# Two layers of memory attention and a spatially gated MLP: the mixer's second tile on ScalarE, w_in's half stored by chunk, the bias rows loaded once, and four moves

## The chip, the cores and the metric

The kernel runs as one program on one core of one Trainium2 chip. The metric is the device time of that program in microseconds, the median of several executions. Beside it stands one profiled execution, whose span and instruction times the trace gives.

## The reference

Two layers, each an attention A and a mixer B, both with a layer norm ahead and a residual sum behind. S = 2048 rows, D = 640, 32 heads of 20, four segments of 512 rows, F = 1728.

```python
# A: per segment s, causal attention inside the segment, plus a memory of the earlier ones
a_dot = softmax(qs @ ks.T * scale + mask) @ vs
a_mem = (phi(qs) @ M) / (phi(qs) @ z + 1e-6)
o     = sigmoid(beta) * a_mem + (1 - sigmoid(beta)) * a_dot
M, z  = M + phi(ks).T @ vs, z + phi(ks).sum(0)
x = x + concat(o) @ wo

# B
z = gelu(layernorm(x) @ w_in)              # 2048 x 1728
z1, z2 = z[:, :864], layernorm(z[:, 864:])
g = w_sp @ z2 + b_sp[:, None]              # w_sp is 2048 x 2048
x = x + (z1 * g) @ w_out
```

## The kernel before

Every float32 matrix product is made of three float16 products: each operand is scaled by a power of two and split into a high and a low half (`split_scaled`, `split_t`), and TensorE adds high x high, high x low and low x high. The scales come from maxima over the weights; `pow2_parts` takes them through TensorE (a transpose `wtp`, then a broadcast `wbc`).

A layer has three stages. **Attention** (0 to some 618 us, and 1183 to 1736) works through pairs of heads, segment by segment: logits (`mp`, `es`), exponentials `P` on ScalarE, their halves `PH` (ScalarE) and `PL` (GpSimd, L1286), products `pv`. Between them run the projections of the tiles to come and, at the end, the output projection `yps` of tiles 0 to 11, whose sum with x is taken out of PSUM by VectorE (L1051). The tiles of x go through `prep(t)`: a load, the statistics, the normalisation, the transpose. **Phase 1b** (618 to 823, 1736 to 1926) takes the 16 row tiles in the order `ORDER` = 0, 8, 1, 9, ...: for tiles 12 to 15 the output projection `yp`, then layer norm, a DMA transpose to `th`, and the two halves of w_in (`zp0` with `wi`, whose result is z1, and `zp1` with `wi1`, whose result is z2). ScalarE takes gelu (L400, L423), VectorE normalises z2, and sums and differences of halves of z2 go to `zh` and `zl`. **Phase 2** (823 to 1180, 1926 to 2277) computes w_sp @ z2 for pairs of row blocks p and p + 8 with seven products in place of eight, after Strassen and Winograd: `gc`, `ga`, `gd`, `gb` are their PSUM banks, `product(ps, q, j, start)` is one product with 24 matmuls, "12", "11", "22", "21" are blocks of w_sp and s1 to s4 sums of them. GpSimd makes the sums (`summed`, L611), ScalarE and VectorE split them (`split`), and ScalarE copies a bank with the bias `bsp` as an addend (`copy`, L708). `gate`, `turn` and `tail` do z1 * g and the product with w_out.

Layer 0 also prepares what layer 1 reuses: split weights are stored to DRAM (`keep`), and the blocks of w_sp's first pair are split during phase 1b (`Rows.first`) and stored as `w0`; `fetch` loads them at the start of phase 2 in both layers. `rows.load(q)` loads the rows of w_sp of one pair, `rows.scales(q)` makes their scales.

Every DMA is issued on SyncE's queue (SP), one after the other: an issue that waits for its data holds all behind it. The order of instructions on each engine comes from a scheduler which follows the code, priorities (`high_priority`) and bounds (`issue_after(x)`: not before x); in phase 2 the order of the four compute engines is that of the code (`manual_schedule`). Each engine then works strictly in that order and waits where data or a buffer is missing.

The lines which the change and the prediction touch: L292 normalises a tile on VectorE, L365 and L366 do the first half of it for tile 0 on VectorE (the negated mean) and ScalarE (x minus mean), and L375 and L376 apply the factor while they split; L335 and L338 load tiles, L377 and L300 transpose them; L162 stores a weight; L468 loads w_sp's rows, L599 is the fetch, L569 loads the bias, L496 and L497 split w_sp's blocks.

Of the kernel before, what the change touches and what calls it, by code (L numbers as in the profile page):

```python
# [20 lines left out]
NT = S // 128  # L21
# [55 lines left out]
def split_scaled(g, h, l, st, c):  # L77

    nc = g.nc
    iv = g.iv[:st.shape[0], c:c + 1]  # L80
    nc.scalar.activation(h, st, AF.Identity, scale=iv)
    nc.vector.scalar_tensor_tensor(l, st, iv, h, ALU.mult, ALU.subtract)

# [84 lines left out]
def prologue(g, ctx, wv, wq, wk, wo, w_in, w_out):  # L168

    nc, tc = g.nc, g.tc  # L170
    wp = ctx.enter_context(tc.tile_pool(name="wqkv", bufs=1))
    g.w = {}
    g.wo = Weight(g, "o", 3, wo, 0, D)
    g.wi = [Weight(g, "i0", 4, w_in, 0, FH), Weight(g, "i1", 5, w_in, FH, FH)]
    g.wu = Weight(g, "u", 6, w_out, 0, D)
    with tc.tile_pool(name="wpro", bufs=1, side="right", reuse_waits="tile") as p, \
            tc.tile_pool(name="wpp", bufs=1, space=PSUM, reuse_waits="tile") as pp:
        st = p.tile([128, KD, D], F32, name="wstv")
        for k in range(KD):
            nc.sync.dma_start(st[:, k, :], wv[k * 128:(k + 1) * 128, :])  # L180
        with tc.high_priority(offset=HP):
            am = p.tile([128, KD], F32, name="wamk")
            for k in range(KD):
                nc.vector.tensor_reduce(am[:, k:k + 1], st[:, k], AX.X, ALU.max, apply_absolute_value=True)
            nc.vector.tensor_reduce(g.wam[:, 0:1], am, AX.X, ALU.max)
            g.vscale = pow2_scales(g, p, pp, "wsc", g.wam, 0, 1)
        g.w["v"] = [wp.tile([128, KD, D], F16, name=f"wv{x}") for x in "hl"]
        g.wqk = {nm + x: nc.dram_tensor(f"w_{nm}{x}", (128, KD, D), F16, kind="Internal").ap() for nm in "qk" for x in "hl"}
        for k in range(KD):
            split_scaled(g, g.w["v"][0][:, k], g.w["v"][1][:, k], st[:, k], 0)  # L190
    g.qk_w = wq, wk
# [53 lines left out]
def other_scales(g, stage, pool, psum, tag):  # L245
# [18 lines left out]
    yield False  # L264
    yield False
    parts = pow2_parts(g, pool, psum, tag, g.wam, 3, 4)
# [49 lines left out]
def phase1b(g, o_d, x, x1_d, z1_d, zh, zl):  # L316

    nc, tc = g.nc, g.tc
    with ExitStack() as ctx:
        pool = lambda n, b, **k: ctx.enter_context(tc.tile_pool(name=n, bufs=b, reuse_waits="tile", **k))  # L320
        pe2, pe1, pe3 = pool("be2", 2), pool("be1", 1), pool("be3", 3)
        wp0, px1, p2, px2, p3 = pool("bw0", 1), pool("bx1", 1), pool("b2", 1), pool("bx2", 1), pool("b1", 3)
        pz1, py, pz0 = pool("bz1", 2, space=PSUM), pool("by", 1, space=PSUM), pool("bz0", 1, space=PSUM)
        g.wi[0].paired(wp0)
        wi0 = g.wi[0].load(g.prep[0], 864, "wr")
# [18 lines left out]
        def attn_out(t, *a):  # L344
# [14 lines left out]
            xn = pe1.tile([128, D], F32, tag="xn", name="xn")  # L359
            if t:  # L360
                layernorm(g, x1, xn, D, 2, XS)
# [69 lines left out]
        for i, t in enumerate(ORDER):  # L431
            if i == 8:
                with tc.issue_after(g.loaded[ORDER[i]].ins):
                    g.wi[0].keep()
            if i + 1 < NT:
# [8 lines left out]
            th = th1  # L444
        z1_half(ORDER[-1], w_in_half(0, *old))
        g.rows = Rows(g)
        if not g.wsp_scaled:
# [107 lines left out]

def phase2(g, b_sp, x1_d, z1_d, zh, zl, out):
    nc, tc = g.nc, g.tc
    KO = 7
    NP = NT // 2
    with ExitStack() as ctx:  # L560
# [6 lines left out]
        woh, wol = g.wu.tiles(wp)  # L567
        bsp = wp.tile([128, NT], F32, tag="bsp", name="bsp")
        nc.sync.dma_start(bsp, b_sp.rearrange("(t p) -> p t", p=128))  # L569
        kn = [128] * 6 + [FH - 768]  # L570
# [21 lines left out]
        def fetch():  # L592
# [3 lines left out]
            with tc.high_priority(offset=HP), tc.issue_after(g.stored.ins):  # L596
                for nm in ("12", "11", "22", "s2", "s1", "s3", "s4"):
                    for c in range(2):
                        nc.sync.dma_start(blocks[0, nm, c], g.w0[nm, c])  # L599

# [87 lines left out]
        bank = lambda nm: pg.tile([128, 512], F32, tag=nm, name=nm)[:, :FHH]  # L688
        fetch()
        with tc.issue_after(g.loaded[ORDER[NT - 1]].ins):  # L690
            rows.load(1)
# [10 lines left out]
        for p in range(NP):  # L702
# [13 lines left out]
            if p:  # L716
                held = gate(over, z1)
                over = turn(p - 1, over, *held)
                split(p, "s1")
                if not q:  # L720
                    split(p, "s4")

# [25 lines left out]
            if p + 2 < NP:  # L748
                rows.load(p + 2)
            if p and q:  # L750
                split(p, "s4")
# [139 lines left out]
class Attention:  # L891
# [78 lines left out]
    def prep(self, t):  # L970
# [7 lines left out]
        def behind():  # L978
            ctx = ExitStack()
            for e in g.hold[:2] if t > 1 else ():  # L980
                ctx.enter_context(self.tc.issue_after(e.ins))
# [368 lines left out]
    def run(self, nseg=NSEG):  # L1350
# [6 lines left out]
        def early():  # L1357
            for t in range(0, 4, 2):

                with self.tc.high_priority(offset=HP if t == 0 else 0):  # L1360
                    for f in zip(self.prep(t), self.prep(t + 1)):
                        f[0]()
# [78 lines left out]
        def background():  # L1441
# [3 lines left out]
            if not g.wo.made:  # L1445
                for i, _ in enumerate(other_scales(g, self.bg, self.pl1, self.pm, "ms")):
                    yield 5 + i if _ else 8 + i
            yield 45
# [81 lines left out]
def interleaved_layers(ctx, tc, x, wq, wk, wv, wo, beta, w_in, w_sp, b_sp, w_out, out):  # L1530
# [4 lines left out]
    attn_consts(g, cp, beta)  # L1535
    prologue(g, ctx, wv, wq, wk, wo, w_in, w_out)

    def dram(name, shape, dt=F32):
# [5 lines left out]
    g.st = [dram(f"st{i}", (D, 3, 2, L), F16) for i in range(2)]  # L1544
    g.w_sp = w_sp
    g.w0 = {(nm, c): dram(f"w0{nm}{c}", (128, 2, 4, 128), F16) for nm in WB for c in range(2)}
    g.hold = ()
    x = rows(x)
    for layer in range(2):
# [5 lines left out]
        with ExitStack() as zs:  # L1555
            with tc.tile_pool(name="topo", bufs=1, side="right", reuse_waits="tile") as to, \
# [7 lines left out]
                phase1b(g, o_d, x, x1_d, z1_d, zh, zl)  # L1564
            phase2(g, b_sp, x1_d, z1_d, zh, zl, x2)
        x = x2
# [26 lines left out]
```

## Time and profile before

| | us |
|---|---|
| median of 3 executions | 2274.4 (2271.16 to 2276.78) |
| the profiled execution | 2279.19 |
| its span in the trace | 2277.5 |
| TensorE busy | 2107.4 |
| VectorE, ScalarE, GpSimd busy | 1606.0, 1250.7, 1458.3 |

The profiled execution is 4.8 us above the median, and 1.7 us of it lie outside the span. The rows of the page that show busy time, and the waits of TensorE, stand in the prediction. A row of the timeline gives start, length, engine, line, operation, and in brackets the idle time just before it with what ended that time; a row of waits gives who waited for whom, the total, how often, and the longest. The granted clock is the share of full speed that TensorE's throttle allowed in a stretch.

### The profile page before, as it was taken

To read this page: it belongs to the slowest core of one execution; us is meant where nothing else is said; L and a number is where in the kernel's file an instruction comes from. 1 tells how busy PE (TensorE), PEld (TensorE's weight loads), DVE (VectorE), ACT (ScalarE), POOL (GpSimd) and SP (SyncE) were. 2 spreads that over 40 slices of the span, in tenths; PEclk is the share of its full clock that TensorE was granted. 3 is DMA by queue.
4 is the path that set the end of the run, shared out by engine and by line. 5 is a ranking of instruction groups with operands and counts; after the bars stand their busy time and mean duration, and the time that the engine had idled before them with its cause. 6 is when DMAs were issued, how large, how long until landed. Compare 5 with 4: busy or idle time off the path is not lost.

```text
span 2277.5 us, 53085 instructions
## 1 busy us (share of the span) xinstructions
PE 2107.4 (93%) x21322; PEld 1266.8 (56%) x21322; DVE 1606.0 (71%) x2761; ACT 1250.7 (55%) x1639; POOL 1458.3 (64%) x1300
## 2 busy tenths in 40 slices
PE   5888888999899989999998998999998999999998
PEld 3455555666554545555554556556664555555555
DVE  7688678677687658878845777786776765576563
ACT  3578688888643433333314887888884333333331
POOL 2387788999844426647611889999996443475560
PEclk9999899999999999999999999999999999999999
DMA  5665557444676678777654447543445336877763
GB/s 164 161 159 157 141 156 174 125 115 124 159 189 180 170 215 208 167 162 187 159 146 117 106 117 178 124 122 89 121 128 149 91 109 197 189 187 174 167 149 84
DMA packets 539639, 342.79 MB, mean 151 GB/s; under 512 B 413536, under 2 KB 465248, under 8 KB 539392
## 3 DMA queue, kind: packets, MB, share of 16 engines
q1 hardware_dynamic: 539392, 339.40, 58.3%
q8 instruction: 167, 2.74, 0.5%
q14 instruction: 80, 0.66, 0.1%
HBM read 159.19 MB, written 92.55 MB: 111 GB/s over the span
## 4 chain that ended last, share of the span: by engine, by line
PE 48%; DVE 16%; POOL 10%; DMA 9%; ACT 8%; issue 6%; SPq 2%; ACTq 0%; DVEq 0%; POOLq 0%
PE zp L387 9%; PE ga L641 9%; POOL PL L1286 6%; PE cyp L677 5%; PE qps L1072 3%; PE pv L1314 3%; PE vps L1013 3%; PE mp L1211 2%; PE kps L1072 2%; PE gb L641 2%; DVE mxs L1275 2%; PE gc L641 2%; ACT PH L1284 2%; PE gd L641 2%; PE es L1211 1%
## 5 line engine op out<-in xcount | busy, mean ns | idle before, releaser
L1286 POOL TENSOR_TENSOR PL<-P,PH 128x640 f16<-128x640 f32 x384 | 539.1, 1429 | 56.0 <-PE pv L1314 44.8
L1275 DVE TENSOR_REDUCE mxs<-mp 128x2 f32<-128x1024 f32 (+2 forms) x384 | 320.5, 862 | 150.0 <-PE mp L1202 148.1
L1249 ACT ACTIVATE P<-es,sc 128x1024 f32<-128x1024 f32 (+1 forms) x256 | 271.3, 1060 | 102.0 <-PE es L1202 91.9
L387 PEld LDWEIGHTS <-th 128*128 128x128 f16 x1920 | 188.1, 98 | 179.7 <-DMA th<-xnhl 11.4
L611 POOL TENSOR_TENSOR ts<-ts,wt 128x512 f32<-128x512 f32 x196 | 280.1, 1440 | 11.1 <-DMA wt<-wn 0.2
L1284 ACT CAST PH<-P 128x1280 f16<-128x1280 f32 x192 | 239.6, 1248 | 1.5
L641 PEld LDWEIGHTS <-wts 128*128 128x128 f16 x1536 | 151.2, 99 | 145.1 <-issue 18.6
L641 PE MATMUL ga<-zh,wts 128*128 128x432 f16 x768 | 214.1, 351 | 11.3 <-ACT u L708 11.2
L286 POOL TENSOR_TENSOR lnrs<-lnve,mhalf 128x1 f32<-128x1 f32 x96 | 60.1, 634 | 247.5 <-DVE lnve L285 234.7
L387 PE MATMUL zp<-wi,th 128*128 128x432 f16 x960 | 183.7, 350 | 5.7 <-ACT z L423 5.7
L1286 POOL TENSOR_TENSOR PL<-Pb,PH 128x640 f16<-128x640 f32 x124 | 175.4, 1438 | 16.0 <-PE pv L1314 14.9
L611 POOL TENSOR_TENSOR ts<-wt,wt 128x512 f32<-128x512 f16 x28 | 34.7, 1241 | 230.6 <-DMA wt<-wn 230.6
L1013 PE MATMUL vps<-wvh,xt 128*128 128x320 f16 x640 | 153.9, 308 | 28.9 <-DVE relu L1104 23.6
L641 PEld LDWEIGHTS <-wt 128*128 128x128 f16 x1152 | 112.5, 98 | 99.6 <-DMA wt<-w 3.3
L677 PE MATMUL cyp<-wuh,ut 128*128 128x320 f16 (+1 forms) x896 | 163.7, 299 | 3.9 <-DMA ut<-un 3.9
L1314 PE MATMUL pv<-vs,PL 128*128 128x41 f16 x2560 | 157.5, 182 | 9.7 <-POOL PL L1286 9.6
L1211 PEld LDWEIGHTS <-qk 64*128 64x128 f16 (+1 forms) x2048 | 78.6, 94 | 155.8 <-issue 135.7
L677 PEld LDWEIGHTS <-ut 128*128 128x128 f16 (+1 forms) x1344 | 131.1, 98 | 58.7 <-DMA ut<-un 5.2
L1314 PE MATMUL pv<-vs,PH 128*128 128x41 f16 x2560 | 160.1, 183 | 0.4 <-DVE ab L1330 0.4
L387 PE MATMUL zp<-wi1h,th 128*128 128x432 f16 x640 | 149.5, 348 | 7.9 <-DMA th<-xnhl 7.6
L1211 PE MATMUL es<-qk 64*128 64x512 f16 (+3 forms) x1024 | 124.8, 300 | 24.6 <-ACT P L1249 20.0
L1314 PEld LDWEIGHTS <-PL 128*128 128x128 f16 x2560 | 140.7, 97 | 11.5 <-POOL PL L1286 11.4
(220 smaller groups left out, 5292.9 us busy)
## 6 DMA issues: line engine op xcount, KB each, us to landing
qk<-st SPq DMA_DIRECT2D x256, 120.0 KB
wr<-in_B_w_sp_dram SPq DMA_DIRECT2D x60, 512.0 KB
z<-z SPq DMA_DIRECT2D x32, 432.0 KB
cz<-z SPq DMA_DIRECT2D x32, 432.0 KB
xt<-in_A_x_dram SPq DMA_DIRECT2D x32, 320.0 KB
st<-qhl SPq DMA_DIRECT2D x40, 256.0 KB
st<-khl SPq DMA_DIRECT2D x40, 256.0 KB
x<-x SPq DMA_DIRECT2D x32, 320.0 KB
```

Of the source, the lines that this page charges most:

```text
L387: nc.tensor.matmul(zp[:, n, :FHH], a[:, k, :], b[:, k, c:c + FHH], start=(k == 0 and j == 0), stop=(k == KD - 1 and j == 2))
L611: nc.gpsimd.tensor_tensor(t, a, t if b == "t" else get(b), ALU.add if op == "+" else ALU.subtract)
L641: nc.tensor.matmul(ps, w[:, a, k % 4, :], z[:, k, j, :], start=start and k == 0 and i == 0, stop=k == NP - 1 and i == 2, skip_group_check= ...
L677: nc.tensor.matmul(yp[:, n, :320], a[:kn[k], k, :], b[:kn[k], k, n * 320:(n + 1) * 320], start=(k == 0 and j == 0), stop=(k == KO - 1 and ...
L1013: nc.tensor.matmul(ps, a[:, k, c], b[:, k, n * 320:(n + 1) * 320], start=(i == 0), stop=(i == 14))
L1072: nc.tensor.matmul(ps, a[:, k, c], b[:, k, :], start=(i == 0), stop=(i == 14))
L1211: nc.tensor.matmul(out[:, h, o:o + w], a[r, ac], b[r, bc], start=o == 0, stop=False, skip_group_check=True)
L1249: g.exp = nc.scalar.activation(P, E, AF.Exp, scale=g.esc)
L1275: e = nc.vector.tensor_reduce(mx[:, :, n, j], mp[:, :, o:o + w], AX.X, ALU.max)
L1284: nc.scalar.copy(PH, P[:, h])
L1286: (nc.gpsimd if h == 0 or n < self.N - self.TAIL else nc.vector).tensor_tensor(PL[:, c], P[:, h, c], PH[:, c], ALU.subtract)
L1314: nc.tensor.matmul(pv[:, i, h, :], x[:, c:c + 128], v[:, j, h0 + h, :], start=(j == 0 and x is PH), stop=(j == i and x is PL), skip_group_ ...
```

## The change

The line numbers of the new kernel are up to 8 higher.

- **Second tile on ScalarE.** In phase 1b, tile 8 takes the way of tile 0: VectorE makes only the negated mean, ScalarE subtracts it, and the factor is applied in the split. Both layers.
- **w_in's half by chunk.** Layer 0 stored w_in's first half in two DMAs behind the ninth tile of the order. Now each of its five chunks of 128 rows is stored (two DMAs each) at the ninth to thirteenth tile.
- **Bias rows once.** `bsp` is loaded once into the constants, instead of in phase 2 of each layer; the code has the load in layer 0's phase 1b, and the order has it as the ninth DMA of the program.
- **Fetch first.** `rows.load(1)` is bound behind the fetch's fourth DMA; SP's order has it behind all fourteen.
- **Last sum's split.** In the last pair, s4 is split where the other pairs have it, behind the copies, instead of ahead of them.
- **Scales' transposes.** `other_scales` yields once less, and its two transposes come some hundred TensorE rows earlier in layer 0's attention.
- **The start.** wv's loads get the priority of x's first tile; `prep(0)` goes ahead of `prep(1)` in layer 0; the statistics of tiles 2 and 3 are bound behind wv's third split.

```diff
@@ prologue
-        for k in range(KD):
-            nc.sync.dma_start(st[:, k, :], wv[k * 128:(k + 1) * 128, :])
+        with tc.high_priority(offset=HP):
+            for k in range(KD):
+                nc.sync.dma_start(st[:, k, :], wv[k * 128:(k + 1) * 128, :])
...
-            split_scaled(g, g.w["v"][0][:, k], g.w["v"][1][:, k], st[:, k], 0)
+            e = split_scaled(g, g.w["v"][0][:, k], g.w["v"][1][:, k], st[:, k], 0)
+            if k == 2:
+                g.third = e
@@ other_scales
     yield False
-    yield False
     parts = pow2_parts(g, pool, psum, tag, g.wam, 3, 4)
@@ phase1b
+        if not g.wsp_scaled:
+            nc.sync.dma_start(g.bsp, g.b_sp.rearrange("(t p) -> p t", p=128))
...
-            if t:
+            if t not in ORDER[:2]:
                 layernorm(g, x1, xn, D, 2, XS)
                 return xn, None
...
-            if i == 8:
+            if 8 <= i < 8 + KD and not g.wi[0].made:
                 with tc.issue_after(g.loaded[ORDER[i]].ins):
-                    g.wi[0].keep()
+                    g.wi[0].keep_chunk(i - 8)
...
+        g.wi[0].made = True
@@ phase2
-        bsp = wp.tile([128, NT], F32, tag="bsp", name="bsp")
-        nc.sync.dma_start(bsp, b_sp.rearrange("(t p) -> p t", p=128))
+        bsp = g.bsp
...
-                        nc.sync.dma_start(blocks[0, nm, c], g.w0[nm, c])
+                        e = nc.sync.dma_start(blocks[0, nm, c], g.w0[nm, c])
+                    if nm == "11":
+                        two = e
+            return two
...
-        fetch()
-        with tc.issue_after(g.loaded[ORDER[NT - 1]].ins):
+        two = fetch()
+        with tc.issue_after(g.loaded[ORDER[NT - 1]].ins), tc.issue_after(two.ins):
             rows.load(1)
...
                 split(p, "s1")
-                if not q:
-                    split(p, "s4")
...
-            if p and q:
+            if p:
                 split(p, "s4")
@@ attention
-            for e in g.hold[:2] if t > 1 else ():
+            for e in (g.hold[:2] or (g.third,)) if t > 1 else ():
...
-                    for f in zip(self.prep(t), self.prep(t + 1)):
+                    with self.tc.high_priority(offset=HP if t == 0 and not self.g.wo.made else 0):
+                        a = self.prep(t)
+                    for f in zip(a, self.prep(t + 1)):
...
-                    yield 5 + i if _ else 8 + i
+                    yield 5 + i
```

How the order moves at three places. First VectorE at the end of layer 0's attention (`xn` is tile 8 normalised, `xt` the drain of `yps`), before:

```order
L1051 SCALAR_TENSOR_TENSOR xt<-yps,sc,xt 128x320
L1325 TENSOR_TENSOR rs<-pv,iomg 128x8
L1326 RECIPROCAL rs<-rs 128x8
L1330 TENSOR_TENSOR ab<-pv,rs 128x328
L292 TENSOR_SCALAR xn<-x_11531,lnmv,lnrs 128x640
L1051 SCALAR_TENSOR_TENSOR xt<-yps,sc,xt 128x320
L1286 TENSOR_TENSOR PL<-Pb,PH 128x640 x2
```

and now:

```order
L369 TENSOR_SCALAR neg<-lnmv 128x1
L1056 SCALAR_TENSOR_TENSOR xt<-yps,sc,xt 128x320
L1330 TENSOR_TENSOR rs<-pv,iomg 128x8
L1331 RECIPROCAL rs<-rs 128x8
L1335 TENSOR_TENSOR ab<-pv,rs 128x328
L1056 SCALAR_TENSOR_TENSOR xt<-yps,sc,xt 128x320
L1291 TENSOR_TENSOR PL<-Pb,PH 128x640 x2
```

The normalisation of tile 8 between the attention's `ab` and the drain is gone; a negation of one column stands earlier, behind the statistics.

Second SP in the middle of layer 0's phase 1b (`w_i0h` and `w_i0l` are the stored halves, `th` the transposed tile), before:

```order
L468 DMA wr<-in_B_w_sp_dram 128x2x512 x2
L424 DMA z_0_9<-z_12017 128x864
L335 DMA x_12187<-x_0_4 128x640
L162 DMA w_i0h<-wi_11498 640x1x864
L162 DMA w_i0l<-wi_11498 640x1x864
L300 DMA_TRANSPOSE th<-xnhl 128x10x128
```

and now:

```order
L473 DMA wr<-in_B_w_sp_dram 128x2x512 x2
L428 DMA z_0_9<-z_12021 128x864
L339 DMA x_12191<-x_0_4 128x640
L152 DMA w_i0h<-wi_11500 128x864
L152 DMA w_i0l<-wi_11500 128x864
L302 DMA_TRANSPOSE th<-xnhl 128x10x128
L345 DMA_TRANSPOSE o<-o_3 128x10x128
L428 DMA z_0_2<-z_12129 128x864
L362 DMA x_0_12<-x_12375 128x640
```

The two whole stores ahead of the transpose have become one chunk's. On TensorE the product of the next tile's `th` with `wi1` (30 matmuls) now stands ahead of the product with `wi` of the tile before; it stood behind 26 of its 30 matmuls.

Third ScalarE in the last pair of layer 0's phase 2 (`wts` are split sums, `u` the copies), before:

```order
L618 CAST wts_16390<-ts_16230 128x512
L665 ACTIVATE un<-u,uivw 128x864
L618 CAST wts_16440<-ts_16259 128x512
L618 CAST wts_16443<-ts_16262 128x512
L618 CAST wts_16446<-ts_16227 128x512
L618 CAST wts_16449<-ts_16230 128x512
L708 ACTIVATE u<-ga,bsp,wsc 128x432 x4
```

and now:

```order
L625 CAST wts_16400<-ts_16240 128x512
L672 ACTIVATE un<-u,uivw 128x864
L625 CAST wts_16450<-ts_16269 128x512
L625 CAST wts_16453<-ts_16272 128x512
L715 ACTIVATE u<-ga,bsp,wsc 128x432 x2
L625 CAST wts_16578<-ts_16237 128x512
L625 CAST wts_16581<-ts_16240 128x512
L715 ACTIVATE u<-ga,bsp,wsc 128x432 x2
```

The second pair of casts (s4) has moved behind two of the copies.

More of the change, by code (lines that the diff above doesn't have):

```diff
@@ L81, in split_scaled @@
     nc.scalar.activation(h, st, AF.Identity, scale=iv)
-    nc.vector.scalar_tensor_tensor(l, st, iv, h, ALU.mult, ALU.subtract)
+    return nc.vector.scalar_tensor_tensor(l, st, iv, h, ALU.mult, ALU.subtract)
 class Weight:
@@ L553, in first, with phase2 @@
         store("s4", 0, 1)
-def phase2(g, b_sp, x1_d, z1_d, zh, zl, out):
+def phase2(g, x1_d, z1_d, zh, zl, out):
     nc, tc = g.nc, g.tc
@@ L1536, in interleaved_layers @@
     prologue(g, ctx, wv, wq, wk, wo, w_in, w_out)
+    g.bsp = cp.tile([128, NT], F32, name="bsp")
     def dram(name, shape, dt=F32):
@@ L1544, in interleaved_layers @@
     g.st = [dram(f"st{i}", (D, 3, 2, L), F16) for i in range(2)]
-    g.w_sp = w_sp
+    g.w_sp, g.b_sp = w_sp, b_sp
     g.w0 = {(nm, c): dram(f"w0{nm}{c}", (128, 2, 4, 128), F16) for nm in WB for c in range(2)}
@@ L1564, in interleaved_layers @@
                 phase1b(g, o_d, x, x1_d, z1_d, zh, zl)
-            phase2(g, b_sp, x1_d, z1_d, zh, zl, x2)
+            phase2(g, x1_d, z1_d, zh, zl, x2)
         x = x2
```

## The prediction

> **What bounds the kernel now.** I read the page first (busy time and the slices), then the waits of TensorE, then its granted clock in the stretches behind the longest waits, and last the timelines of the places that the change touches.
>
> ```profile
> span 2277.5 us, 53085 instructions
> PE 2107.4 (93%) x21322; PEld 1266.8 (56%) x21322; DVE 1606.0 (71%) x2761; ACT 1250.7 (55%) x1639; POOL 1458.3 (64%) x1300
> ```
>
> TensorE works 2107.4 of 2277.5 us, so some 170 us are its idle time, and no edit here takes matmuls away. A saving can only come from its waits, and from the clock behind them. The waits, by what ended them:
>
> ```profile
> PE ga L641 <- ACT u L708: 11.2, 9, 3.8
> ...
> PE yps L1045 <- DVE xt L1051: 8.5, 2, 5.4
> ```
>
> Columns: total us, times, longest. These two groups are 19.7 us in 11 waits; the change touches their longest ones, and single waits of other groups shown below at their places. Behind several of them TensorE also runs slowly (start:end, length, busy, granted clock, DMA share, GB/s):
>
> ```profile
> 612.00:618.00 6.00, 4.32 (x46) 0.72 0.57 154
> 693.50:701.00 7.50, 7.42 (x27) 0.65 0.90 226
> 823.00:827.50 4.50, 4.42 (x25) 1.00 1.05 392
> 845.00:851.00 6.00, 5.92 (x24) 0.72 0.47 87
> 1137.00:1144.30 7.30, 7.14 (x26) 0.63 0.01 2
> 1727.00:1733.00 6.00, 5.13 (x55) 0.51 0.80 166
> ```
>
> Length times (1 - clock) is what the slow clock cost there: 1.7, 2.6, 0, 1.7, 2.7 and 2.9 us. The wait before 823 was 2.85 us (its row stands below) and left the clock at 1.00; those before the others were 3.08 to 5.67 us. So a long wait that is removed returns about 2 us beyond its length.
>
> [...]
>
> **Second tile centred on ScalarE, layers 0 and 1.**
>
> ```profile
> 603.40 9.77 DVE L292 TENSOR_SCALAR xn<-x,lnmv,lnrs 128x640 f32<-128x640 f32 x1 [0.32 <-POOL lnrs L286]
> 609.65 2.75 POOL L1286 TENSOR_TENSOR PL<-Pb,PH 128x640 f16<-128x640 f32 x2
> 613.68 0.42 PE L1045 MATMUL yps<-woh,o 128*128 128x320 f16 x1 [3.08 <-DVE xt L1051]
> 615.99 1.42 SPq L377 DMA_TRANSPOSE th<-xnhl  x1
> 620.22 0.90 PE L387 MATMUL zp<-wi1h,th 128*128 128x432 f16 x2 [1.81 <-DMA th<-xnhl]
> 1716.96 10.40 DVE L292 TENSOR_SCALAR xn<-x,lnmv,lnrs 128x640 f32<-128x640 f32 x1 [1.69 <-POOL lnrs L286]
> 1727.87 0.42 PE L1045 MATMUL yps<-woh,o 128*128 128x320 f16 x1 [5.45 <-DVE xt L1051]
> 1729.77 2.76 POOL L1286 TENSOR_TENSOR PL<-Pb,PH 128x640 f16<-128x640 f32 x2 [0.53 <-PE pv L1314]
> L292 DVE TENSOR_SCALAR xn<-x,lnmv,lnrs x30: 606/612/10396, 603.4 to 1909.9; 128x640 f32<-128x640 f32 x30
> L366 ACT ACTIVATE xn<-x,neg x2: 828/830/833, 537.0 to 1654.8; 128x640 f32<-128x640 f32 x2
> ```
>
> The same normalisation that takes 0.61 us in the median took 9.77 and 10.40 us for tile 8, while GpSimd ran one subtraction after the other, and it ended when they did. The PSUM drain L1051 stood behind it on VectorE, and TensorE waited for that. The change replaces it by L366 on ScalarE (0.83 us) and a tiny negation on VectorE. ScalarE's 0.83 us stands in its queue of exponentials and casts; it worked 55% of the span, and GpSimd's chain, not ScalarE, ends last there: I take 0, bound 0.8 a layer, its own length.
>
> In layer 0 the wait of 3.08 us goes, but GpSimd's own chain still runs to 612.4, and tile 0's transpose was issued at 615.99 and ended TensorE's wait 4.2 us later. TensorE had been ready for the drain at 610.6 (613.68 - 3.08). With the drain at about 611 and the transpose, behind two more drains' stores, at about 613, the first w_in matmul starts near 617 in place of 620.2: 3.1 us, plus some of the clock. I take 3.5 (2 to 5.5). In layer 1 GpSimd's last part began at 1729.77, since it waited for a `pv` behind the same stall; it can begin near 1727, when GpSimd had no other work left (the 10.40 us end at 1727.4), so 2.8 us earlier. The drains and the last `pv` behind it ran at half the clock for 2.9 us of loss, which goes too, less a little: attention ends about 5.3 us earlier (3.5 to 6.5). Next late there: GpSimd's subtractions.
>
> **w_in's half stored by chunk.**
>
> ```profile
> 682.15 1.44 SPq L162 DMA_DIRECT2D w_i0l<-wi  x1
> 683.70 6.74 SPq L300 DMA_TRANSPOSE th<-xnhl  x1
> ...
> 693.58 7.41 PE L387 MATMUL zp<-wi,th 128*128 128x432 f16 x26 [5.67 <-ACT z L423]
> ```
>
> Two stores of 1080 KB (the row is the second) stand ahead of the transpose, whose issue then took 6.74 us. TensorE stood in front of the first-half product of the tile before, which waits for ScalarE's L423. Now one fifth of the stores stands there, and TensorE's order has the second-half product of the next tile first, which needs only the transpose. That lands near 690 (bounds 688 to 691: 683.7, the 4.2 us above, and what the stores and loads still ahead take), and that product covers L423: 26 matmuls took 7.41 us, 4.8 without the slow clock, so its 30 take 5.6. The stall cost 5.67 + 2.6 = 8.3 us; about 2.1 stay; gain 6.2 (3 to 8). The other eight issues on SP are at most 1.4 us each (1.44 above, for five chunks) and go past loads of tiles to come; one pair goes ahead of w_in's last load, which that delays by its issue: 0, bound -1.
>
> **Bias once, and the fetch ahead of the rows.**
>
> ```profile
> 812.80 2.78 SPq L468 DMA_DIRECT2D wr<-in_B_w_sp_dram  x3
> 815.62 4.37 SPq L599 DMA_DIRECT2D wt<-w  x6
> 823.08 0.36 PE L641 MATMUL gc<-zh,wt 128*128 128x432 f16 x1 [2.85 <-DMA wt<-w]
> ...
> 822.38 1.22 DVE L480 TENSOR_REDUCE am<-wr 128x1 f32<-128x1024 f32 x1
> ...
> 827.20 2.56 ACT L496 ACTIVATE wn<-wr,wsc 128x512 f16<-128x512 f32 x4 [1.12 <-DMA wts<-w0s]
> ...
> 844.32 0.71 ACT L708 ACTIVATE u<-ga,bsp,wsc 128x432 f32<-128x432 f32 x1 [9.46 <-DMA bsp<-in_B_b_sp_dram]
> 845.08 0.34 PE L641 MATMUL ga<-zh,wts 128*128 128x432 f16 x1 [3.21 <-ACT u L708]
> ```
>
> With the fetch some 2.8 us earlier and no w_sp megabytes before it, the 2.85 us go. ScalarE's copy waited 9.46 us for the bias alone: 3.21 us of TensorE and 1.7 of clock, 4.9. What is late next is the copy's place on ScalarE: four casts of w_sp stand ahead of it, and their rows now load behind fourteen fetch issues. The fetch, fourteen blocks of 128x1024 in 2 bytes, is 3.7 MB, which at the 392 GB/s of the row at 823 is 9.4 us; the rows, 2.1 MB, 5.3 us more, so from 812.8 they land near 829, some latency included. Before, the last reduction of the rows began at 822.38 and the casts were through at 829.8, 7.4 us later; so now near 837. TensorE, without its 2.85 and 3.21 us, asks for the copy's result at 845.1 - 6.1 = 839.0, so for its start by 838. I keep 4.9 (bounds 2.5 and 5). In layer 1, of the 11.2 us of `ga <- ACT u`, little can be here: 3.21 and the 3.79 below are layer 0's, and the other seven are 4.2 together. I take 0.5 (0 to 1).
>
> **Last sum's split.**
>
> ```profile
> 1130.29 1.12 ACT L618 CAST wts<-ts 128x512 f16<-128x512 f32 x2
> ...
> 1135.88 0.62 ACT L618 CAST wts<-ts 128x512 f16<-128x512 f32 x1 [2.51 <-POOL ts L611]
> 1136.41 0.70 ACT L708 ACTIVATE u<-ga,bsp,wsc 128x432 f32<-128x432 f32 x1
> 1137.16 0.52 PE L641 MATMUL ga<-zh,wts 128*128 128x432 f16 x1 [3.79 <-ACT u L708]
> ```
>
> The copy stood behind casts that wait for GpSimd's sum. In front of them, behind the two casts at 1130.29, it runs at about 1131.5, before the `gd` product ended (1137.16 - 3.79 = 1133.4). 3.79 + 2.7 = 6.5 us go (5 to 6.7). The sum is ready at 1135.9; its product comes after two other products (25 such matmuls took 4.42 us at 823) and a tail of 42 matmuls, which cover the split. In layer 1, by the same seven, I take 0.
>
> **The start and the scales.** wv's five loads now go before the second tile, and VectorE takes their reductions first.
>
> ```profile
> 13.97 0.37 PE L60 MATMUL wtp<-ident,wam 128*1 128x128 f32 x1 [9.61 <-DVE wam L185]
> ...
> 22.00 0.42 PE L1013 MATMUL vps<-wvl,xt 128*128 128x320 f16 x1 [2.56 <-DVE wvl L82]
> 226.46 0.27 PE L60 MATMUL wtp<-ident,wam 128*4 128x128 f32 x1 [2.34 <-DVE gm L1150]
> ```
>
> One load less ahead is about 0.9 us, and tiles 2 and 3 behind the third split free most of 2.56 us; against it stand their later transposes, and the bias load, whose issue took 0.39 and 1.10 us:
>
> ```profile
> L569 SPq DMA_DIRECT2D bsp<-in_B_b_sp_dram x2: 388/742/1096, 839.1 to 1940.3; - x2
> ```
>
> It stands ahead of the first transpose of x, under the 9.61 us that TensorE waits for `wam`; without that cover it costs its 1.1 us. For the start I take +1.5 (-3 to +4). The scales' transposes lose a wait of 2.34 us and meet another at their new place; 0 (-2 to +3.5), in the middle, since the trace shows no wait for VectorE at the new place that names its price.
>
> **Sum.** 3.5 + 5.3 + 6.2 + 2.9 + 4.9 + 0.5 + 6.5 + 1.5 = 31.3 us. Not all of it reaches the end. In layer 0 TensorE comes almost 10 us earlier into the tiles after 700, where VectorE is nearly full, and one wait there hangs on its chain:
>
> ```profile
> 748.50 0.87 DVE L356 SCALAR_TENSOR_TENSOR x<-yp,sc,xt 128x640 f32<-128x640 f32 x1
> ...
> 757.92 0.54 PE L387 MATMUL zp<-wi1h,th 128*128 128x432 f16 x2 [2.03 <-DMA th<-xnhl]
> ```
>
> I take 5 us as given back, 3 there and 2 in small waits of TensorE elsewhere: 26 net. Against the profiled execution (2279.2 us, span 2277.5 and 1.7 around it) that is 2253. That execution stood 4.8 above the median of 2274.4, so for the median I forecast 2248.5.
>
> **Rivals.**
> 1. The tiles of layer 0 give the gain back: TensorE, earlier by 9.7 us, only waits longer at 757.92, because the chain from 748.50 does not move. For it speaks VectorE's dense stretch; against it that the chain begins with a product that itself comes earlier. All of 9.7 lost in place of 3: 2274.4 - 26 + 6.7 = 2255.
> 2. Another VectorE instruction is caught behind GpSimd at the end of attention, as L292 was: the new two-input split of tile 8, or the last drains. Then 8.8 us are lost: 2257. [...] Against it: that split of tile 0 (L376) took 1.32 us in both layers.
> 3. The start and the moved scales cost 5 together in place of giving 1.5: 2255.
> 4. Slower: the w_sp rows land so late that the sums of every later pair of row blocks slip with them, at the copy L708 and on GpSimd. Each us past 830 costs one there; the whole gain is used up from 26 us late on, and at 34 the time is 2282. Fourteen issues and 3.7 MB in front give 7 us, not 26, so this is far off.
> 5. More than the sum: nothing is given back, and the waits at 690 and 620 vanish too: 2238 to 2242.
>
> **Numbers.** Forecast 0.55; rival 1 0.15; rival 2 0.08; rival 3 0.08; rival 5 0.08; a mixture of 1 to 3 that ends within 0.3% (6.8 us, about what this measurement tells from no change) 0.04; slower 0.02. Faster is then 0.94. The range of 2240 to 2264 takes in rivals 1 to 3 and half of 5.
>
> **What would show it.** Right: L292 has no instruction over 2 us; no TensorE wait over 3 us between 600 and 1180; `ga <- ACT u` falls from 11.2 to some 5 us with only the 0.8 us ones left; `gc <- DMA wt` is gone; the clock is 1.00 behind all these places. Wrong: a wait `zp <- DMA th` over 5 us in the tiles after 700, a first copy L708 that waits for VectorE's scales, or a longer stretch before 55 us.

## The result, and the profile after

| | us |
|---|---|
| changed kernel, median of 4 executions | 2244.86 (2243.81 to 2252.05) |
| kernel before, 4 executions beside it | 2272.78 (2271.13 to 2276.78) |
| ratio | 0.9881, 95% interval 0.9856 to 0.9907 |
| the profiled execution of the changed kernel | 2244.01 |

The change makes the kernel about 27 us faster. The forecast of 2248.5 against 2274.4 is a ratio of 0.9886. Beginning and busy times of the changed kernel's page:

```profile
span 2242.3 us, 53105 instructions
PE 2096.5 (93%) x21322; PEld 1264.6 (56%) x21322; DVE 1598.1 (71%) x2761; ACT 1253.1 (56%) x1641; POOL 1463.0 (65%) x1300
```

TensorE is busy 10.9 us less with the same 21322 matmuls, which fits the mean granted clock of the span, 0.983 before and 0.988 now, and the rest of the 35.2 us between the two spans is waiting. Its waits in the changed kernel (total us, times, longest):

```profile
PE zp L391 <- DMA th<-xnhl: 6.9, 6, 2.4
PE pv L1319 <- DVE ab L1335: 5.9, 2, 2.9
...
PE ga L648 <- ACT u L715: 3.7, 4, 1.8
```

`gc <- DMA wt`, `yps <- DVE xt` and `zp <- ACT z` are gone from the list, `ga <- ACT u` has fallen from 11.2 to 3.7 us, and a group has come up in the second row: two waits of 2.9 us for `ab`, one in each layer (`ab` is VectorE's product of `pv` with `rs`, the output of a pair of heads). The timeline of the changed kernel at the places of the prediction, in order of time:

```profile
601.55 2.81 POOL L1291 TENSOR_TENSOR PL<-Pb,PH 128x640 f16<-128x640 f32 x2
602.28 3.92 DVE L1291 TENSOR_TENSOR PL<-Pb,PH 128x640 f16<-128x640 f32 x2 [6.05 <-PE pv L1319]
606.77 1.45 SPq L381 DMA_TRANSPOSE th<-xnhl  x1
607.53 0.18 PE L1319 MATMUL pv<-vs,PH 128*128 128x41 f16 x1 [2.93 <-DVE ab L1335]
610.73 0.90 PE L391 MATMUL zp<-wi1h,th 128*128 128x432 f16 x2 [2.01 <-DMA th<-xnhl]
681.71 0.54 PE L391 MATMUL zp<-wi1h,th 128*128 128x432 f16 x2 [2.39 <-DMA th<-xnhl]
742.53 0.54 PE L391 MATMUL zp<-wi1h,th 128*128 128x432 f16 x2 [1.01 <-DMA th<-xnhl]
821.68 0.70 ACT L715 ACTIVATE u<-ga,bsp,wsc 128x432 f32<-128x432 f32 x1
853.63 1.01 ACT L672 ACTIVATE un<-u,uivw 128x864 f16<-128x864 f32 x1 [9.07 <-DVE uivw L665]
856.84 0.34 PE L648 MATMUL ga<-zh,wts 128*128 128x432 f16 x1 [1.82 <-ACT u L715]
1106.18 0.71 ACT L715 ACTIVATE u<-ga,bsp,wsc 128x432 f32<-128x432 f32 x1 [0.40 <-DVE un L673]
1703.74 0.18 PE L1319 MATMUL pv<-vs,PH 128*128 128x41 f16 x1 [2.93 <-DVE ab L1335]
```

The instructions by line, changed kernel (count, then ns: least, median, most):

```profile
L294 DVE TENSOR_SCALAR xn<-x,lnmv,lnrs x28: 605/612/1539, 624.7 to 1874.4; 128x640 f32<-128x640 f32 x28
L1291 DVE TENSOR_TENSOR PL<-Pb,PH x4: 810/1998/3186, 602.3 to 1701.6; 128x640 f16<-128x640 f32 x4
```

and the kernel before:

```profile
L1286 DVE TENSOR_TENSOR PL<-Pb,PH x4: 808/815/826, 613.6 to 1733.6; 128x640 f16<-128x640 f32 x4
```

No normalisation is longer than 1.54 us any more. But VectorE's own share of the last subtractions, which before came after GpSimd had ended, now runs beside it, and the first of the two in each layer takes some 3.2 us in place of 0.81 (602.28 in the timeline, beside GpSimd's pair at 601.55).

The clock in the stretches that answer to those of the prediction (start:end, length, busy times by engine, granted clock, DMA share, GB/s):

```profile
611.00:619.00 8.00, 8.00 (x33) 3.82 (x32) 6.53 (x6) 4.07 (x6) 2.51 (x2) 0.72 0.98 232
684.00:691.50 7.50, 7.50 (x43) 4.02 (x42) 7.50 (x13) 3.93 (x6) 4.02 (x3) 1.00 0.59 175
805.00:809.50 4.50, 4.50 (x26) 2.44 (x25) 3.91 (x4) 2.13 (x4) 3.84 (x4) 1.00 1.05 387
821.60:827.60 6.00, 6.00 (x34) 3.23 (x33) 3.20 (x5) 2.23 (x4) 0.00 (x0) 1.00 0.80 182
1106.80:1114.10 7.30, 7.30 (x43) 3.97 (x42) 3.00 (x3) 0.30 (x2) 3.35 (x3) 1.00 0.29 65
1704.00:1711.00 7.00, 7.00 (x62) 3.86 (x59) 1.72 (x5) 0.72 (x1) 3.59 (x5) 0.76 0.79 245
```

It is 1.00 behind the chunked store, the fetch, the first copy and the last pair's copy. It is still 0.72 and 0.76 at the end of the two attentions. Of the prediction's other signs, no wait of TensorE between 600 and 1180 us is over 3 us, if narrowly (2.93), and one wait for the copy is 1.82 us, above the 0.8 that were to stay.

Both kernels run the same matmuls on TensorE in nearly the same order, so the start of the n-th matmul can be compared. Changed minus before, us:

| time in the kernel before | shift | what lies between |
|---|---|---|
| 98 | -4.4 | the start |
| 211 | +4.4 | attention, the scales' new place |
| 608 | -8.1 | the rest of layer 0's attention |
| 663 | -9.2 | end of attention, first tiles |
| 708 | -14.4 | the chunked store |
| 798 | -15.4 | tiles to the end of phase 1b |
| 861 | -23.5 | fetch and first copy |
| 896 | -21.5 | the second pair's copy |
| 1132 | -23.9 | the pairs between |
| 1155 | -30.4 | the last pair's copy |
| 1714 | -29.6 | layer 1's attention |
| 1789 | -32.6 | its end, first tiles |
| end | -35.2 | layer 1's phases 1b and 2 |

From 608 us on that is 27.1 us, which is the median's gain. The 8.1 us before it are another matter: the six kernels below with the code of before in layer 0's attention stand 0 to 6.8 us earlier at 608 than the one trace of before, and a second trace of the changed kernel stands 1.3 us earlier there (and gains 27.9 us behind it).

### The profile page after: what moved, and what is told of

The parts are those of the page before. It is cut to its first block, busy times and chain, and to the rows that moved or that the text cites. A ratio compares the mean times of both kernels' runs of the same rounds, so it can differ in the third digit from the quotient of the medians.

```text
span 2242.3 us, 53105 instructions
## 1 busy us (share of the span) xinstructions
PE 2096.5 (93%) x21322; PEld 1264.6 (56%) x21322; DVE 1598.1 (71%) x2761; ACT 1253.1 (56%) x1641; POOL 1463.0 (65%) x1300
## 4 chain that ended last, share of the span: by engine, by line
PE 60%; DVE 11%; POOL 10%; ACT 8%; issue 5%; DMA 5%; SPq 1%; DVEq 0%; ACTq 0%; POOLq 0%
PE zp L391 12%; PE ga L648 12%; PE cyp L684 7%; POOL PL L1291 7%; PE gb L648 3%; PE vps L1018 3%; PE qps L1077 3%; PE pv L1319 3%; PE gc L648 3%; PE gd L648 3%; PE mp L1216 2%; PE kps L1077 2%; ACT PH L1289 2%; DVE mxs L1280 2%; ACT P L1254 2%
## 5 line engine op out<-in xcount | busy, mean ns | idle before, releaser
L618 POOL TENSOR_TENSOR ts<-ts,wt 128x512 f32<-128x512 f32 x196 | 282.4, 1452 | 11.0
L1018 PE MATMUL vps<-wvh,xt 128*128 128x320 f16 x640 | 156.0, 311 | 27.9 <-DVE relu L1109 21.4
L618 POOL TENSOR_TENSOR ts<-wt,wt 128x512 f32<-128x512 f16 x28 | 34.5, 1233 | 224.5 <-DMA wt<-wn 224.5
L1319 PEld LDWEIGHTS <-PH 128*128 128x128 f16 x2560 | 139.1, 96 | 16.3 <-issue 6.5
```

Source lines behind the costliest of these rows:

```text
L618: nc.gpsimd.tensor_tensor(t, a, t if b == "t" else get(b), ALU.add if op == "+" else ALU.subtract)
L1018: nc.tensor.matmul(ps, a[:, k, c], b[:, k, n * 320:(n + 1) * 320], start=(i == 0), stop=(i == 14))
L1319: nc.tensor.matmul(pv[:, i, h, :], x[:, c:c + 128], v[:, j, h0 + h, :], start=(j == 0 and x is PH), stop=(j == i and x is PL), skip_group_ ...
```

## The experiments

Each kernel's median is compared with executions of the kernel before on the same chip. "Place by place" means the shift of TensorE's matmuls in the trace, as in the table above. That is a comparison with one trace of before, so the other traces with the same code at a place show how far it scatters there. In the expectations, "the second pass" is phase 2 and its "first gather" the first product, `gc`.

**Tile 8 on ScalarE, alone** (the kernel before with this edit):

```diff
-            if t:
+            if t not in ORDER[:2]:
                 layernorm(g, x1, xn, D, 2, XS)
```

> The kernel before with one part of the change: the mixer's second tile centred on ScalarE. By the prediction's terms (3.5 + 5.3 us) the time falls by 8.8 us. Rival, from the trace of the changed kernel: a VectorE subtraction PL (0.81 us alone) is held 3.2 us at the same place while GpSimd runs, TensorE waits 2.9 us for what stands behind it, and the part is worth only some 4 us: 1.3 in layer 0 and 2 to 3 in layer 1.

Measured: 2273.4 us, ratio 0.9996 (0.9983 to 1.0009): -0.9 us, no difference. Its lines and its timeline:

```profile
L1286 DVE TENSOR_TENSOR PL<-Pb,PH x4: 809/1996/3189, 604.3 to 1723.4; 128x640 f16<-128x640 f32 x4
```

```profile
609.53 0.18 PE L1314 MATMUL pv<-vs,PH 128*128 128x41 f16 x1 [2.94 <-DVE ab L1330]
613.04 0.90 PE L387 MATMUL zp<-wi1h,th 128*128 128x432 f16 x2 [2.33 <-DMA th<-xnhl]
```

Place by place it gains 0.2 us in layer 0 and some 2.5 to 3 us in layer 1, against 3.5 and 5.3 forecast; that is nearer the rival. Even the 0.2 is no gain: between 608 and 663 us this trace gains 0.5 us, and six traces with tile 8 still on VectorE gain 0.8 to 1.4 there against the same trace of before. The 3.08 us wait for the drain is replaced by 2.94 us for `ab`, behind the held subtraction, and the transposed tile is then waited for 2.33 us in place of 1.81.

**The chunked store, alone.**

```diff
-            if i == 8:
+            if 8 <= i < 8 + KD and not g.wi[0].made:
...
-                    g.wi[0].keep()
+                    g.wi[0].keep_chunk(i - 8)
```

> The kernel before with one part: w_in's half stored by chunk. By the prediction's term 6.2 us less, and the wait zp <- ACT z of 5.7 us gone, a wait for th of 2 to 2.5 us in its place. Rival (the tiles after give it back): 3 us less or none, with the wait for th that stood at 757.92 grown from 2.0 to 5 us or more.

Measured: 2273.48 us, ratio 0.9985 (0.9973 to 0.9997): -3.4 us. Place by place -4.7 us from 663 to 708 us and -0.7 more by 798, so 5.4 of the 6.2 forecast; some 2.4 us are lost again by layer 1, where its code is that of before. The median alone would fit the rival's 3 us, but the wait that the rival needs is not there: at the place of 757.92 it is 1.36 us (2.03 before).

**Bias once and fetch first, together.** The edit is the diff's parts on `bsp`, `two` and `fetch()`.

> The kernel before with two parts: the bias rows loaded once, and w_sp's rows loaded behind the fetch. By the prediction's terms 4.9 + 2.9 + 0.5 = 8.3 us less. Rival (the rows come too late for the first copy L708): 5 us less or fewer, with a wait ga <- ACT u over 1 us at the first copy of layer 0's phase 2.

Measured: 2262.28 us, ratio 0.9947 (0.993 to 0.9964): -12.0 us. Place by place -3.0 at the first `gc` and -5.05 at the first copy (forecast 2.9 and 4.9), +1.8 at the second pair's copy, and about -1.7 in layer 1.

**The fetch first, alone.**

```diff
-        fetch()
-        with tc.issue_after(g.loaded[ORDER[NT - 1]].ins):
+        two = fetch()
+        with tc.issue_after(g.loaded[ORDER[NT - 1]].ins), tc.issue_after(two.ins):
             rows.load(1)
```

> The kernel before with the fetch moved ahead only (the rows of w_sp for the second pass asked for first), without the single load of the bias rows. Together the two gave 3.0 us at the second pass's first gather and 5.05 at its first copy in layer 0's trace. Theory (each wait has its own cause): the fetch alone takes the gather's wait of about 3 us and nothing else in layer 0, and the wait of about 3.2 us at the first copy for the bias rows stays: 2.5 to 3.5 us in the trace, ratio 0.9985 to 0.999. Rival (an earlier fetch also clears the queue for the bias rows): the first copy's wait goes too, 6 to 8 us, ratio 0.9965.

Measured: 2279.11 us, ratio 1.0013 (1.0002 to 1.0025): 3 us slower, which neither theory had. Its timeline, at the first copy in layer 0 and in layer 1:

```profile
835.03 0.71 ACT L711 ACTIVATE u<-ga,bsp,wsc 128x432 f32<-128x432 f32 x1 [3.80 <-DMA bsp<-in_B_b_sp_dram]
835.80 0.52 PE L644 MATMUL ga<-zh,wts 128*128 128x432 f16 x1 [4.60 <-ACT u L711]
...
1912.87 0.63 SPq L468 DMA_DIRECT2D wr<-in_B_w_sp_dram  x1
...
1927.39 6.59 SPq L502 DMA_TRANSPOSE wt<-wn  x4
1934.07 0.54 SPq L569 DMA_DIRECT2D bsp<-in_B_b_sp_dram  x1
1938.27 0.52 PE L644 MATMUL ga<-zh,wts 128*128 128x432 f16 x1 [5.41 <-ACT u L711]
```

and SyncE in layer 1 of the kernel before:

```profile
1880.63 2.81 SPq L468 DMA_DIRECT2D wr<-in_B_w_sp_dram  x4
...
1928.41 5.12 SPq L502 DMA_TRANSPOSE wt<-wn  x3
...
1940.26 0.39 SPq L569 DMA_DIRECT2D bsp<-in_B_b_sp_dram  x1
```

The wait of `gc` is gone, but TensorE, earlier, waits 4.60 us at the copy in place of 3.21: 0.5 us is left of 3.0. In layer 1 the rows of w_sp were asked for at 1880.63, ahead of the fetch; now they come behind it, from 1912.87 on. Their first four transposes stand ahead of the bias load on SyncE in both kernels, and they are now late and hold it: measured against TensorE's matmuls it is issued some 6 us later than before. A wait of 5.41 us appears where the kernel before had none; with the slower matmuls behind it (0.52 and 0.56 us, where the changed kernel's at 823.24 took 0.35) it costs 7.9 us, 1.3 of which the trace had gained just ahead of it. So the two edits don't add up: with the fetch moved, the single load of the bias is worth 0.0066 of the time, 15 us (+-5), by the two ratios (some 14 place by place).

**The last sum's split, alone.** The edit is the two places of the diff with `split(p, "s4")`.

> The kernel before with one part: the last sum's split behind the copies. By the prediction's term 6.5 us less, all in layer 0's last pair: 3.8 of waiting and 2.7 of slow clock. Rival (only the waiting goes, the clock recovers by itself): 3.8 us less.

Measured: 2269.7 us, ratio 0.9973 (0.9958 to 0.9987): -6.1 us (3.0 to 9.6, which does not exclude the rival's 3.8). Place by place it is -6.5 at the last pair's copy, the forecast's figure, and that is more than the wait. Five of six traces without this edit stand 1.0 to 1.6 us better there than the one of before, so some 5.5 us is the nearer figure.

**The start and the scales, alone.** The edit is the diff's parts in the prologue, `other_scales` and `attention`.

> The kernel before with two parts: the start (wv first, statistics of tiles 2 and 3 behind the third split) and the scales' transposes moved. By the prediction's terms 1.5 us less (-4.5 to +5 the bounds). Rival, from the first profile of the changed kernel, which stood 8 us ahead after 400 us: 8 us less. Third possibility: executions of one and the same code differ by some us in layer 0's attention, and those 8 us are mostly that; then about 2 us less.

Measured: 2273.36 us, ratio 0.9999 (0.9986 to 1.0012): nothing. Place by place -5.6 us at 98 us, -0.5 at 211, and -6.1 again at 608, which the median does not bear out. All traces together say more. From 98 to 211 us, where the scales now stand, the seven traces with these parts lose 5.0 to 8.7 us; the seven without them range from a gain of 1.2 to a loss of 3.6. At 608 the seven with them stand 1.3 to 8.0 us ahead of the one trace of before (4.7 in the mean), the seven without 0 to 6.8 (2.5 in the mean). That is the third possibility. No run separates the start from the scales.

**The changed kernel, measured again.**

> The changed kernel once more, for a sharper ratio and as the measure for the variants beside it. The prediction has -26 us (ratio 0.9886); its first measurement was 0.9881 with an interval of 0.9856 to 0.9907. If the start and the scales' transposes are worth 8 us, as the first profile seems to say, rather than 1.5, the ratio is near 0.985.

Measured: 2250.0 us, ratio 0.9886 (0.9864 to 0.9908). The parts' own medians add up to -22.6 us (0.9, 3.4, 12.0, 6.1, 0.2), each to about 3 to 4 us, the sum so to about 7; the whole is -26 to -27. The parts are additive within that, which leaves room for some us either way.

**What holds VectorE's instruction?** The kernel before, with tile 8's normalisation on VectorE in another form: two tensor inputs from SBUF in place of one.

```diff
+            if t == ORDER[1]:
+                mv, rs = layernorm_stats(g, x1, D, 2, XS)
+                nc.vector.scalar_tensor_tensor(xn, x1, mv[:, 0:1],
+                    rs.to_broadcast((128, D)), ALU.subtract, ALU.mult)
+                return xn, None
```

> The kernel before with one instruction changed: tile 8's normalisation stays on VectorE, but as a scalar_tensor_tensor with two SBUF inputs (the factor spread over the 640 columns) in place of a tensor_scalar with one. Theory: the one-input form alone is held until GpSimd is idle, the two-input form shares; it then takes 0.8 to 3.2 us in place of 9.8 and 10.4, and the time falls as in the kernel with tile 8 on ScalarE (0 to 4 us less). [...]

Measured: ratio 1.0002 (0.999 to 1.0015). The form makes no difference:

```profile
L362 DVE SCALAR_TENSOR_TENSOR xn<-x,lnmv,lnrs x2: 10101/10410/10720, 601.4 to 1710.6; 128x640 f32<-128x640 f32 x2
```

```profile
601.44 10.10 DVE L362 SCALAR_TENSOR_TENSOR xn<-x,lnmv,lnrs 128x640 f32<-128x640 f32 x1
611.47 0.54 DVE L1055 SCALAR_TENSOR_TENSOR xt<-yps,sc,xt 128x320 f32<-128x320 f32 x1
```

One input or two, it takes some 10 us: 9.77 and 10.40 in the kernel before, 10.10 and 10.72 here, where the theory had 0.8 to 3.2. In the kernel before, in layer 0, GpSimd's row beside it, which is mostly subtractions, ran from 603.35 to 612.82, and L292 from 603.40 to 613.17:

```profile
603.35 2.75 POOL L1286 TENSOR_TENSOR PL<-P,PH 128x640 f16<-128x640 f32 x2
...
612.35 0.47 POOL L1334 TENSOR_TENSOR gm<-ab 128x160 f32<-128x160 f32 x1
```

So it was not the form of L292 that made the long instruction.

**GpSimd's last subtractions on VectorE** (the changed kernel with this edit):

```diff
-            (nc.gpsimd if h == 0 or n < self.N - self.TAIL else nc.vector)
+            (nc.gpsimd if n < self.N - self.TAIL else nc.vector)
                 .tensor_tensor(PL[:, c], P[:, h, c], PH[:, c], ALU.subtract)
```

> The changed kernel, and GpSimd's subtraction PL for the very last pair of heads goes to VectorE, so that no GpSimd work runs beside VectorE's last two. Theory (VectorE's PL is held 3.2 us by GpSimd, and TensorE's wait of 2.9 us hangs on it): the wait in front of the last pv falls below 2 us in both layers, the clock stays up, and the time is 3 to 7 us below the changed kernel's. Rival: VectorE's four subtractions in a row last as long as GpSimd's two beside one held (3.2 + 0.8 us), and nothing changes.

Measured: 2250.0 us, ratio 0.989 (0.9871 to 0.9908): as the changed kernel. Its lines and its timeline in layer 1:

```profile
L1291 DVE TENSOR_TENSOR PL<-Pb,PH x8: 809/810/4058, 604.1 to 1702.5; 128x640 f16<-128x640 f32 x8
```

```profile
1695.15 0.32 SPq L1058 DMA_DIRECT2D x<-xt  x1
1703.41 0.32 SPq L342 DMA_DIRECT2D xt<-x  x1
1703.78 1.33 SPq L381 DMA_TRANSPOSE th<-xnhl  x1
...
1709.40 0.90 PE L391 MATMUL zp<-wi1h,th 128*128 128x432 f16 x2 [3.55 <-DMA th<-xnhl]
```

The longest still takes 4.06 us, the median is 0.81, and the wait for `ab` falls from 2.93 to 1.69 us in both layers, as the theory had it; the clock did not stay up (0.62 from 611 to 619 us). What is late next is the transpose of tile 0: on SyncE a load of another tile stands ahead of it (L342), which could go only at 1703.41, when VectorE was through with its subtractions (the last began at 1702.5). In layer 0 the first 26 matmuls of `zp` take 7.26 us behind waits of 1.69 and 2.13 (4.90 with both edits, below); in layer 1 the first 30 take 8.61, behind 1.69 and 3.55.

**The transpose ahead of that load** (the changed kernel with this edit):

```diff
+            with tc.issue_after(g.th0.ins):
                 g.loaded[t] = nc.sync.dma_start(xt, x[t])
...
-                nc.sync.dma_start(th..., hl..., transpose=True)
+                e = nc.sync.dma_start(th..., hl..., transpose=True)
+                if not g.gelu:
+                    g.th0 = e
```

> The changed kernel; only the loads of the MLP's first input tiles that SyncE issues at the end of attention are bound to come behind the transpose of token tile 0's output, instead of ahead of it. In the changed kernel that transpose (th) was issued at 606.77 us in layer 0, behind a load that had waited for VectorE, and the first projection (zp) waited 2.01 us for it right after the 2.93 us wait at VectorE's accumulation; its 30 matmuls then took 7.97 us instead of 5.65. Theory 1 (two waits close together make the slow clock): without the th wait the projection starts right behind the accumulation, and its 30 matmuls take under 6.5 us; gain 2 to 3.5 us against the changed kernel in layer 0, 0 to 1 in layer 1. Theory 2 (the 2.93 us wait alone makes the slow clock): the th wait of 2.01 goes, the 30 matmuls still take 7 to 8 us; gain about 2. Rival: the loads that now stand behind are late for the MLP, and the gain is given back within two tiles: no difference. Ratio against the kernel before: 0.986 to 0.988 by theories 1 and 2, 0.9886 by the rival.

Measured: 2248.17 us, ratio 0.9879 (0.9858 to 0.99), which alone does not tell it from the changed kernel. The timeline in layer 0:

```profile
601.31 1.68 SPq L382 DMA_TRANSPOSE th<-xnhl  x1
609.83 0.20 PE L1322 MATMUL pv<-vs,PH 128*128 128x41 f16 x1 [2.93 <-DVE ab L1338]
611.22 0.89 PE L394 MATMUL zp<-wi1h,th 128*128 128x432 f16 x2
```

The transpose goes 5.5 us earlier (7.8 against the same matmul of TensorE), the second wait is gone, and the 30 first matmuls of `zp` take 6.29 us in place of 7.97: 3.5 us at once, 2.8 after two tiles. In layer 1, which had no such wait, nothing is left of a gain. That is what theory 1 has, in one trace; the places listed at the end of this document bear it out, though the slowest of them with the 2.9 us wait alone (7.02 us) would fit theory 2.

**Both together.**

> The kernel with the transpose ahead of the loads, as in the run before it, and beside it the last head pair's share of the split of probabilities that GpSimd did is done on VectorE, as in the earlier run where that alone brought nothing. There the wait at the accumulation fell from 2.93 to 1.69 us in both layers, and in layer 1 a wait of 3.55 us for the transpose took its place, since SyncE's load ahead of it waited 7.86 us for VectorE. Theory: with the order turned, that wait is gone too, so both layers keep 1.2 us and lose the slow clock: 4 to 7 us against the changed kernel, ratio to the kernel before 0.9855 to 0.987. Rival: the lost time at the end of attention is set by VectorE's work as a whole, and comes back as a wait for VectorE in the first MLP tiles: 0 to 2 us, ratio 0.988 or more.

Measured: 2243.17 us, ratio 0.9854 (0.9839 to 0.9869), as the theory had it, and the fastest kernel here; its interval still touches those of the changed kernel. Timeline and windows in layer 0:

```profile
611.46 0.18 PE L1322 MATMUL pv<-vs,PH 128*128 128x41 f16 x1 [1.69 <-DVE ab L1338]
612.49 0.53 PE L394 MATMUL zp<-wi1h,th 128*128 128x432 f16 x2
```

```profile
611.00:619.00 8.00, 7.54 (x76) 4.58 (x77) 6.91 (x10) 5.07 (x6) 3.81 (x5) 1.00 0.64 200
```

Full clock behind the wait, and the 30 matmuls take 5.63 us. Place by place the end of attention is 4.7 us better than in the changed kernel in layer 0 and 0.8 in layer 1; 1.9 us of it go at the second pair's copy.

**Chunks one tile later** (the changed kernel, `i - 9` in place of `i - 8`):

> The changed kernel with each chunk of the store issued one token tile later. The changed kernel still waits 2.39 us for a transposed tile (th) at 681.71, the first tile beside which a chunk is stored. Theory (the chunk stands ahead of that transpose on its queue or shares the DMA engines with it): one tile later, that wait shrinks by 1 to 2 us, gain about 1.5 us, ratio 0.988. Rival 1: the wait moves to the next tile with the chunk: no difference, 0.9886. Rival 2: the last chunk is now too late for the second pass's gather: a wait there of 1 to 5 us, ratio 0.989 to 0.991.

Measured: 2244.73 us, ratio 0.9863 (0.9847 to 0.9879). The trace does not bear out the theory: the wait at its tile is 2.06 us in place of 2.39, and place by place the kernel stands the same 1.8 us behind the changed one ahead of the store and behind it. A ratio some 0.002 lower without a place for it is what such a ratio leaves open between two builds.

## Why the prediction was right, and where it was not

The net figure came out because two errors cancelled: a term that was too large by some 6 to 8 us, and a deduction of 5 us that was mostly not needed where it was put. That 26 came so close to 27 is in part luck.

- **Tile 8, 3.5 + 5.3: the step that failed.** The step was "attention ends about 5.3 us earlier", and in layer 0 that the drain's wait goes. The single run shows 0.2 at most and 2.5 to 3 in the trace, and -0.9 us (+-3) by the median. The prediction took GpSimd's subtractions as next late and their length as given. It did not ask what VectorE's own subtraction does when it, in place of L292, stands beside GpSimd's: 3.2 us in place of 0.81. This is rival 2 in part, at a place it did not name, since it looked at the split and the drains. Whether its 3.19 us and the 9.77 and 10.40 of L292 have one cause no run here shows.
- **The clock behind it.** "1.00 behind all these places" failed at the two ends of attention: a wait of 2.93 us followed by one of 2.01 leaves 0.72, and 2.93 alone left 0.76 in layer 1.
- **The chunked store, 6.2:** right in place and nearly in size (4.7 alone and 5.1 in the whole at the store, 5.4 and 6.1 by 798 us); the remaining 2.39 us wait at 681.71 is the "about 2.1" that was to stay. Of the gain the single run's median shows 3.4 (0.7 to 6.1).
- **Fetch 2.9 and bias 4.9:** right as a pair (8.1 at these places in the single run and in the whole), wrong as two terms. The fetch alone loses. That its wait would only move to the copy, and that in layer 1 the late rows and their transposes would hold the bias load behind them, was not seen. Layer 1 gave about 1.7, not 0.5.
- **The last split, 6.5:** right, and exact against the one trace of before (6.1 by the median). The copy began at 1106.18, 3.1 us before the product that needs it (1109.3).
- **Start and scales, 1.5:** 0.2 +-3. The sum was right, its two parts were not: the start gave more than 1.5 (1.7 to 5.6 us at 98 us, where traces without it stand between 2.1 earlier and 0.1 later), and in the stretch where the scales now stand, put at 0, it was lost again.
- **Given back, 5:** wrong place. The wait at 757.92 did not grow, it shrank to 1.01 (742.53). What came back was 1.8 us at the second pair's copy (856.84): ScalarE there stood in the 9.07 us wait for VectorE's `uivw`, with the casts and the copy behind it.
- **Rivals 1, 3 and 4** did not come. w_sp's rows were in time: the copy at 821.68 ran without a wait of its own and began 1.6 us ahead of its product. The margin was thin: the casts of the rows ahead of it had started only at 819.22, just behind VectorE's scales, and it ended 0.9 us ahead of the product.

The trace's -35.2 us overstate the gain: 8.1 of it is in layer 0's attention, where the single kernels with unchanged code scatter by 6.8 and two traces of the changed kernel by as much.

## What to carry to other kernels

When a held instruction is removed, ask which instruction now stands in its place beside the same engine, and price that one as held too: here L292's 9.77 and 10.40 us went, and a subtraction of 0.81 us took 3.19. Before a DMA is moved ahead on a queue, list what falls behind it in every pass over the same code, and check whether two edits share one wait: their terms are then worth something together and may cost alone (here -12.0 us for the pair and some 3 us more for the fetch alone). The slow clock behind a removed wait can return too, but look at what takes the wait's place: here the clock went from 0.65, 0.72 and 0.63 to 1.00 behind the chunked store, the first copy and the last pair's copy, and was still 0.72 and 0.76 at the ends of the attentions, where waits of 2.93 us had come, in layer 0 with one of 2.01 behind it. And one trace is not a baseline: look at several traces with the same code before a few microseconds at a place are called a gain.

## What the runs showed of the hardware

At the end of attention, VectorE's instructions that work from SBUF to SBUF were not slowed a little but held beside GpSimd's row of subtractions: in the kernel before 9.77 and 10.40 us with one tensor input (0.61 in the median of L292), in the changed kernel 3.19 and 3.18 for a subtraction that takes 0.81 alone. At the same place the form with two tensor inputs took 10.10 and 10.72 us, and with all of GpSimd's last subtractions on VectorE the longest took 4.06. They ended shortly after the row's last instruction, L292 0.35 and 0.36 us and the subtractions 0.68: in the changed kernel a GpSimd product (L1339, below) ends that row at 604.79, and the held subtraction ends at 602.28 + 3.19 = 605.47. The drains that read PSUM (L1056) took 0.50 to 0.55 us in all 48 cases, 43 of them beside GpSimd's work.

Not every row of GpSimd holds like this, nor every read of SBUF. Rows of the changed kernel:

```profile
604.26 0.53 POOL L1339 TENSOR_TENSOR gm<-ab 128x160 f32<-128x160 f32 x1
L285 DVE BATCH_NORM_STATS2 lnst<-xt x64: 439/476/496, 3.8 to 1495.6; 128x6 f32<-128x320 f32 x64
L626 DVE TENSOR_TENSOR wts<-ts,wts x112: 676/1430/1670, 842.2 to 2202.3; 128x512 f16<-128x512 f32 x112
L618 POOL TENSOR_TENSOR ts<-ts,wt x196: 1146/1484/2022, 830.5 to 2187.7; 128x512 f32<-128x512 f32 x196
844.23 1.49 POOL L618 TENSOR_TENSOR ts<-ts,wt 128x512 f32<-128x512 f32 x1
844.63 2.00 DVE L673 SCALAR_TENSOR_TENSOR un<-u,uivw,un 128x864 f16<-128x864 f32 x1
```

The statistics of attention's tiles (L285), which read one SBUF tensor, never took over 0.50 us, though half of them (33 of 64) began beside a GpSimd instruction of over 1 us. In phase 2 GpSimd is busy too, for 148 of the 245 us from 850 to 1095, but there VectorE's subtractions of two SBUF tensors (L626) come through in 1.43 us in the median: 0.68 where nothing of GpSimd runs beside them (26 of 112), 1.64 beside it (69), 1.67 at most. GpSimd's own sums (L618) take 1.49 us in the median beside VectorE and 1.16 without it. Both are longer beside each other, and neither lasts as long as the other's row: five sums ran from 841.43 to 849.21, and the L673 of the rows above took 2.00 us in the midst of them. Why it is otherwise at the end of attention stays open.

The slow clock behind a wait of 2.93 us is not certain. After such a wait alone the 30 first matmuls of `zp` took 5.63, 6.27, 6.29, 6.41 and 7.02 us in five places of four profiled runs; with a wait of 2.0 to 2.3 us close behind it, 7.97, 8.00 and 8.18; after 1.69 us alone 5.63 and 5.64. What sets these places apart no run here shows.
